# Sliding-window attention and spectral mixing on one core: ACT fills half of the late banks of the tail, and the first halves of four weight groups are read in 8 KB runs

## The chip, the cores and the metric

The kernel runs on one core of one Trainium2 chip. The metric is the device time of one execution in microseconds (us). Before the change it is 430.06 us, the median of three runs (429.9 to 430.35). A profiled execution of the same kernel took 430.23 us; its instructions span 428.4 us of that.

## The reference

Two operators follow each other, on eight batches of 576 tokens, eight heads of 64 (512 channels in all).

```python
mask = (rel >= 0) & (rel < 64)                 # each token sees itself and 63 before it
x = softmax(where(mask, q @ k.T / 8, -1e9)) @ v     # heads side by side: [8, 576, 512]
X = rfft(x, axis=1)[:, :64]                    # 64 modes of the sequence
Yr = Xr @ w_r - Xi @ w_i;  Yi = Xr @ w_i + Xi @ w_r  # each mode its own 512 x 512 matrices
y = irfft(Y, n=576)
u = x + y
out = u + maximum(u @ w_ch, 0)
```

The mode weights w_r and w_i are 64 matrices of 1 MB each in fp32, 134 MB together. All of them have to be read once.

## The kernel before, in words

**Order of the work.** The program is written out by hand in issue order for each engine (`tc.manual_schedule()`); semaphores come from the use of tiles. In the first stage, attention runs over 40 units (lines 510 to 545): PE turns q, k and v (L298, L310), makes scores (L337, L345), subtracts the maximum (L357), turns the probabilities (L365) and multiplies by v (L385). A DFT of each batch (L408) leaves X in `XQ[0]` (first 256 channels) and `XQ[1]` (other 256).

**Weights.** POOL issues every weight load as a DMA that casts fp32 to bf16 (`load_weights`, lines 157 to 215). The 16 groups have four modes each. Groups 0 to 9 come in halves of 256 input channels: `steps` first has the first halves (hb = 0) of groups 0 to 9, then their second halves, then groups 10 to 15 by pairs of modes with all 512 channels. A load of a half group and of w_r or w_i has 1 MB after the cast. Usually one DMA brings it (L203), with two rows of 512 numbers side by side for each partition and mode: 4 KB read, 2 KB written in a run. For the second halves of groups 2 to 9 (`WIDE = 2`), two DMAs of 512 KB bring it (L195), each of two modes, with four rows side by side: 8 KB read, 4 KB written. The other form needs X with the channels spread in another way over the partitions: `wide_modes` (lines 721 to 745) does that for `XQ[1]` with matmuls by a spread identity, and leaves it in `XE`. The loads go into rings of tiles (`ringA`, `ringB`, of three and five buffers), into `Yall` and into some lent tiles. POOL issues them in order, among the raw loads of q, k and v (L285), and a load waits for its buffer to be spent by PE.

**Mode matmuls.** `mode_half` (L223) has 8 matmuls for w_r and 8 for w_i, four of them side by side on PE in 32 columns each. `mode_wide` (L235) also has 8 and 8, two side by side in 64 columns each. The first halves (L223, in `early_step`, lines 536 to 543) run inside the attention stage, in its iterations 22, 23, 24, 26, ... 38; ACT keeps their sums in `Yacc` (L542). After attention, the second halves and then the pairs of groups 10 to 15 (`mode_pair`, L254) run as their weights land, with the product x w_ch (`x_jobs`) and the inverse DFT of what is complete between them.

**The tail.** When the last weights have landed, 36 output tiles of 128 tokens are left, as 18 pairs in the list `seq`. Pairs of the first four batches (list `AA`, "early") have their sums over all modes but the last prepared in `UE`, and need only 32 rows for the last modes (`late_z` L986, `late_u` L979). The others (list `BB`, "late") need all modes (`rows_z` L1050, `rows_u` L1021). `X4` are two late pairs with the last 64 tokens of two batches in one tile; their u matmuls are in two column halves (L1027), their last modes in 32 rows (L1047, L1033). A round of the last loop (lines 1195 to 1198) does for pair n on PE: put x w_ch into two banks (`tail_xw`, L966, a matmul by the identity), add z (`summed`); ACT takes the relu in place (L1074); then for pair n-1 PE adds u into the same bank, DVE adds what is missing and writes the output tile (L1085, L1039), and SP sends it (L996). There are four sets of two banks.

**Warm-up.** PE starts with `WARM` = 59 small matmuls on zeros (L432) while the first k and q are loaded.

Of the kernel before, what the change touches and what calls it, by code (L numbers as in the profile page):

```python
# [16 lines left out]

NRA = 3
NRB = 5
WARM = 59  # L20
NEG = -1.0e30
MAGIC = 12582912.0
PSAFE = 3.14159
# [3 lines left out]
def kernel(  # L27
# [75 lines left out]
    XA = XA[:, 0:(3 * NW + 2) * B * NMF].rearrange("p (s b m) -> p s b m", b=B, m=NMF)  # L103
    steps += [(grp, hb) for grp in (*range(EARLY, LAST), *range(LAST + 2, NGRP), LAST, LAST + 1) for hb in range(2)]
    WIDE = 2
    NE = 2 * (EARLY - WIDE)
    SHARES = 25, 11, 80, 12
    assert sum(SHARES) == 128
    XE = XE[:, 0:(7 * NW + 2) * B * NE].rearrange("p (s b m) -> p s b m", b=B, m=NE)
    ONES = 3, 0  # L110
    wlist = []
    for at, (grp, hb) in enumerate(steps):
# [37 lines left out]
    def load_weights(n):  # L150
        nonlocal nload
        while nload < len(wlist):
            at, parts, hb, ri = wlist[nload]
            if 2 * n <= sum(len(ps) for ps in parts):
                return
            if nload in lent:
                w = lent[nload]
            else:
                open_to = "a" if at >= 2 * EARLY else "aby" if at < EARLY + 2 else "ab"
                h = min(open_to, key=lambda h: held[h][0] if len(held[h]) == room[h] else -1)  # L160
                if len(held[h]) == room[h]:
                    if held[h][0] not in spent:
                        return
                    held[h].pop(0)
                held[h].append(nload)
                if h == "y":
                    w = lentY
                else:
                    w = {"a": ringA, "b": ringB}[h].tile([128, 4, NJ, DM], BF16, name="wi" if ri else "wr", tag="wt")
            src = moe_w_i if ri else moe_w_r  # L170
            if at >= 2 * EARLY:
                w = w.rearrange("p (m h) j e -> p m (h j) e", m=2)
                p = parts[0][0]
                if nload == wstart[2 * EARLY]:
                    row = 0
                    for i, size in enumerate(SHARES):
                        for m in [slice(0, 2)] if i < 2 else [slice(0, 1), slice(1, 2)]:
                            nc.gpsimd.dma_start(
                                out=w[row:row + size, m],
                                in_=src[p:p + 2][m].rearrange("m (p j) e -> p m j e", j=NW)[row:row + size])  # L180
                        row += size
                else:
                    for m, k, lo, hi in ((0, 1, 0, NW), (1, 1, 0, NJ), (1, 1, NJ, NW)) if nload == len(wlist) - 1 else ((0, 2, 0, NW),):
                        nc.gpsimd.dma_start(  # L184
                            out=w[:, m:m + k, lo:hi],
                            in_=src[p + m:p + m + k].rearrange("m (p j) e -> p m j e", j=NW)[:, :, lo:hi])
                wtiles.update(((p + m, ri), w[:, m]) for m in range(2))
                nload += 1
                n -= 2
                continue  # L190
            if at >= EARLY + WIDE:
                w = w.rearrange("p (q h) j e -> p q (h j e)", q=2)
                for i in range(2):
                    p = parts[0][2 * i]
                    nc.gpsimd.dma_start(  # L195
                        out=w[:, i], in_=src[p:p + 2, HALF:DM, :].rearrange("h (p j) e -> p h (j e)", j=NW))
                    wtiles[p, hb, ri] = w[:, i].rearrange("p (j e) -> p j e", j=NW)
                nload += 1
                n -= 4
                continue  # L200
            to = 0
            for ps in parts:
                nc.gpsimd.dma_start(  # L203
                    out=w[:, to:to + len(ps)],
                    in_=src[ps[0]:ps[-1] + 1, HALF * hb:HALF * hb + HALF, :].rearrange("g (p j) e -> p g j e", j=NJ))
                for i, p in enumerate(ps):
                    wtiles[p, hb, ri] = w[:, to + i]
                to += len(ps)
            nload += 1
            n -= to  # L210
# [20 lines left out]
    def mode_wide(psm, at, ri):  # L231
        grp, hb = steps[at]
        for j in range(NW):
            for i in range(2):
                nc.tensor.matmul(out=psm[64 * i:64 * i + 64, :],  # L235
                                 lhsT=XE.rearrange("k s b m -> k (s b) m")[:, (7 * j + 1 - ri) * B:(7 * j + 9 - ri) * B,
                                                                           2 * (grp - WIDE) + i],
                                 rhs=wtiles[4 * grp + 2 * i, hb, ri][:, j], start=(ri == 0 and j == 0),
                                 stop=(ri == 1 and j == NW - 1), tile_position=(0, 64 * i))
        for i in range(2):  # L240
            wtiles.pop((4 * grp + 2 * i, hb, ri))
        spend(at, ri)

    def mode_pair(psm, at, ri):
        grp, h = steps[at]
# [16 lines left out]
    with tc.manual_schedule():  # L262
# [2 lines left out]
        trigF = maskp.tile([128, NTF, 2 * NM], BF16, name="trigF")  # L265
        mask_t = maskp.tile([128, 3, 4, 128], BF16, name="mask_t")
        rawp = pool("rawp", bufs=2)
        qtp = pool("qtp", bufs=3)
        vtp = pool("vtp")
        vdp = pool("vdp")  # L270
# [264 lines left out]
        def early_step(it):  # L535
            nonlocal step
            grp = step
            psm = ps_m.tile([128, DM], FP32, name="psm", tag="misc")
            for ri in range(2):
                mode_half(psm, grp, ri)  # L540
                load_weights(due(it) - loaded())
            nc.scalar.copy(out=Yacc[grp], in_=psm)  # L542
            step += 1
# [55 lines left out]
        trigX = zpool.tile([128, 128], BF16, name="trigX")  # L599
        trigXr = zpool.tile([128, 128], FP32R, name="trigXr")  # L600
        XL = zpool.tile([128, 3 * NW + 2, B, 8], BF16, name="XL")
        sprE = XL.rearrange("p s b m -> p (s b m)")[:, 0:512].rearrange("p (r h k) -> p r h k", r=2, h=2)
        trpool = pool("trpool", bufs=2, reuse_waits="tile")

        banks = {"m": pool("ps_mc", bufs=2, space=PSUM, reuse_waits="tile"),
# [113 lines left out]
                    nc.vector.tensor_scalar(out=XA[:, i], in0=px[:, 1], scalar1=-1.0, scalar2=None, op0=ALU.mult)  # L719

        def wide_modes():
            nc.vector.memset(sprE, 0.0)
            for r in range(2):
                for h in range(2):
                    nc.vector.tensor_copy(out=sprE[:, r, h, h::2], in_=ident_bf[:, r::2])
            pts = [[bank("zt"[r == 0]) for j in range(NJ)] for r in range(2)]
            for r in range(2):
                for j in range(NJ):
                    for h in range(2):
                        nc.tensor.matmul(  # L730
                            out=pts[r][j][:, 2 * B * NE * h:2 * B * NE * (h + 1)], lhsT=sprE[:, r, h],
                            rhs=XQ[1][:, 3 * j + 1:3 * j + 3, :, 4 * WIDE:4 * EARLY].rearrange(
                                "p t b (m h) -> p (t b) m h", h=2)[:, :, :, h],
                            start=(h == 0), stop=True, skip_group_check=True)
            nc.vector.memset(XE[:, 0:7 * NW].rearrange("p (j s) b m -> p j s b m", s=7)[:, :, 3], 0.0)
            nc.vector.memset(XE[:, 7 * NW:], 0.0)
            for r in range(2):
                for j in range(NJ):
                    i = 7 * (NJ * r + j)
                    px = pts[r][j].rearrange("p (h t b m) -> p h t b m", h=2, t=2, b=B)  # L740
                    xe = [XE[:, i + t:i + t + 8].rearrange("p (h s) b m -> p h s b m", h=2) for t in range(2)]
                    nc.scalar.copy(out=xe[1][:, :, 0:2], in_=px)
                    nc.vector.tensor_scalar(out=xe[0][:, :, 0], in0=px[:, :, 1], scalar1=-1.0, scalar2=None, op0=ALU.mult)
            lo = 4 * (LAST - EARLY)
            nc.vector.tensor_copy(out=XL, in_=XA[:, :, :, lo:lo + 8])

# [205 lines left out]
        BB = [(8, 17), (26, 35)] + [(i, i + 1) for k in range(NLB // 2, B // 2) for i in range(9 * k, 9 * k + 8, 2)]  # L952
        assert sorted(i for p in AA + BB for i in p) == list(range(NT))
        X4 = [BB.pop(0) for _ in range(2)]
        seq = [AA.pop(0) for _ in range(4)]
        while AA:
            seq += [BB.pop(0), AA.pop(0)]
        seq += X4 + BB
        ps, pu = {}, {}
        plan = [i for n, p in enumerate(seq) for i in (p if n else p[::-1])]  # L960
        done = {}

        def tail_xw(n, js=(0, 1)):
            for i in [seq[n][j] for j in js]:
                ps[i] = bank(("tt", "yp", "zz", "mm")[n % 4][seq[n].index(i)])
                nc.tensor.matmul(out=ps[i], lhsT=ident_r, rhs=XW[i], start=True, stop=True)  # L966

        def banks_u(n, of):
            for j, i in enumerate(seq[n]):
# [225 lines left out]
        for n in range(2, end):  # L1195
            tail_xw(n)
            summed(n)
            added(n - 1)
        banks_u(end, ("tt", "yp", "zz", "mm")[(end + 1) % 4])
        ut = new_ut()  # L1200
# [39 lines left out]
```

## Time and profile before

| what | before |
|---|---|
| median of three runs | 430.06 us |
| the profiled execution | 430.23 us |
| its span, first to last instruction | 428.4 us |
| PE busy | 336.4 us (79%) |
| DVE busy | 245.7 us (57%) |
| ACT busy | 185.7 us (43%) |
| POOL busy | 90.6 us (21%) |
| moved by all DMA queues | 93.29 MB, mean 218 GB/s |
| weights' queue (software, from POOL) | 31424 packets, 81.80 MB |
| HBM read | 163.58 MB |
| chain that ended last | DMA 49%, PE 37%, issue 4%, DVE 4%, ACT 4%, POOL 1% |

The page of the profile lists busy times, the span in 40 slices (each 10.7 us), the queues, the chain that ended last, the costliest groups and the DMA issues. Bytes of a casting DMA are counted as written (bf16). In the timeline and in the chain, the columns are the start in us from the first instruction, the length in us, engine, line and tiles; what stands in brackets is how long the engine stood idle before and what ended that. In groups, the last number of "x8 | 4.3, 582" is the mean length of one in ns. A windows row gives the stretch, each engine's busy us with the number of instructions, the granted PE clock, the share of the DMA engines and GB/s.

### The profile page before, as it was taken

The page shows a single profiled execution, that of the slowest core. Times are in us where ns is not written, and L with a number is a line of the kernel's source. Part 1 is how long each engine was busy: PE and PEld are TensorE (multiplying, and loading weights), DVE is VectorE, ACT ScalarE, POOL GpSimd, SP SyncE. Part 2 cuts the span into 40 slices and gives each one's busy share as a digit, 9 for nine tenths or more (in the row PEclk, how much of TensorE's full clock was granted, in tenths as well). Part 3 has the DMA queues.
Part 4 walks back from the last instruction along what each step waited for, and adds up shares of the span by engine and source line. Part 5 has one row for each costly group of instructions (what it writes and reads, how often), then busy time and mean ns, then how long its engine had stood idle before and what let it go on. Part 6 is the DMA issues. An engine that isn't in the chain of part 4 may idle for free.

```text
span 428.4 us, 11528 instructions
## 1 busy us (share of the span) xinstructions
PE 336.4 (79%) x5000; PEld 226.7 (53%) x5043; DVE 245.7 (57%) x525; ACT 185.7 (43%) x337; POOL 90.6 (21%) x156
## 2 busy tenths in 40 slices
PE   6898999898999988976627567668676767878994
PEld 5676767676667766662315334345454545445442
DVE  8498887778677765785402212133322334885886
ACT  6575757575676657533301101124222213323772
POOL 8222213122122132112222222211111111120200
PEclk8699999999999999996656888689998998999998
DMA  8999999999999999999999999999999999996797
GB/s 202 212 212 211 211 212 211 212 211 211 211 212 211 212 212 212 211 213 214 213 251 222 213 214 214 206 215 215 214 214 215 215 214 214 214 211 117 264 356 283
DMA packets 37187, 93.29 MB, mean 218 GB/s; under 512 B 2992, under 2 KB 3248, under 8 KB 37136
## 3 DMA queue, kind: packets, MB, share of 16 engines
q0 software_dynamic: 31424, 81.80, 97.8%
q1 hardware_dynamic: 5568, 10.62, 6.8%
q8 instruction: 39, 0.64, 0.5%
q10 hardware_dynamic: 144, 0.13, 0.1%
q14 instruction: 12, 0.10, 0.1%
HBM read 163.58 MB, written 9.44 MB: 404 GB/s over the span
## 4 chain that ended last, share of the span: by engine, by line
DMA 49%; PE 37%; issue 4%; DVE 4%; ACT 4%; POOL 1%; DVEq 0%; ACTq 0%; POOLq 0%
DMA wr<-in_moe_w_r_dram 26%; DMA wi<-in_moe_w_i_dram 23%; PE tr L298 5%; PE s L345 4%; PE s L357 4%; PE pt L365 3%; PE vb L310 3%; PE o L385 2%; PE s L337 2%; PE psz L685 2%; PE psm L254 1%; DVE xw L890 1%; PE psm L223 1%; DMA vd<-in_k_dram 1%; PE px L408 1%
## 5 line engine op out<-in xcount | busy, mean ns | idle before, releaser
L685 PE MATMUL psz<-wch,tr 128*128 128x512 f32 x176 | 57.8, 457 | 10.8 <-DMA wch<-in_moe_w_ch_dram 10.1
L944 DVE CAST xw<-psz 128x512 fp32r<-128x512 f32 x36 | 24.9, 692 | 68.6 <-PE psz L685 68.1
L349 DVE TENSOR_REDUCE mx<-s 128x4 fp32r<-128x512 f32 x72 | 49.4, 687 | 24.7 <-PE s L345 24.4
L653 ACT CAST tr<-ptx 128x512 fp32r<-128x512 bf16 x36 | 21.2, 590 | 80.4 <-PE ptx L678 80.4
L359 ACT ACTIVATE p<-s 128x512 bf16<-128x512 f32 x72 | 39.7, 603 | 12.4 <-PE s L357 12.4
L685 PEld LDWEIGHTS psz<-wch,tr 128*128 128x128 f32 x176 | 34.2, 215 | 17.4 <-issue 10.3
L345 PE MATMUL s<-kT,qT 64*64 64x128 bf16 (+1 forms) x576 | 29.5, 223 | 6.9 <-issue 6.9
L302 ACT COPY kT<-tr 128x576 bf16<-128x576 bf16 x32 | 23.2, 724 | 23.8 <-PE tr L298 23.8
L235 PEld LDWEIGHTS <-XQ 128*64 128x64 bf16 x128 | 14.1, 203 | 30.7 <-issue 25.1
L345 PEld LDWEIGHTS <-qT 64*64 64x64 bf16 x576 | 18.3, 108 | 18.1 <-issue 17.6
L302 ACT COPY qT<-tr 128x576 bf16<-128x576 bf16 x32 | 23.3, 728 | 10.0 <-PE tr L298 10.0
L368 DVE COPY pts<-pt 128x1024 bf16<-128x1024 bf16 (+1 forms) x40 | 25.2, 629 | 3.9 <-PE pt L365 2.3
L357 PE MATMUL s<-mx,ident_r 128*128 128x512 f32 x72 | 26.9, 445 | 0.1
L254 PEld LDWEIGHTS <-XQ 128*32 128x32 bf16 x256 | 9.2, 150 | 29.8 <-issue 29.7
L302 ACT COPY vT<-tr 128x576 bf16<-128x576 bf16 x32 | 23.3, 727 | 3.4 <-PE tr L298 3.3
L749 DVE TENSOR_TENSOR stg<-psm,Yfour 128x512 bf16<-128x512 f32 x10 | 6.9, 691 | 30.4 <-PE psm L235 27.3
L235 PE MATMUL psm<-wi,XQ 128*64 128x512 bf16 x64 | 13.6, 494 | 12.2 <-DMA wi<-in_moe_w_i_dram 12.2
L365 PE MATMUL pt<-ident_bf,p 128*128 128x128 bf16 x288 | 23.0, 221 | 0.2 <-DVE pts L368 0.2
L397 DVE TENSOR_TENSOR x_sb<-o,r 128x512 bf16<-128x512 f32 x32 | 22.1, 692 | 1.1
L285 POOL DMA_DIRECT2D rawk<-in_k_dram x15 | 8.1, 538 | 65.1 <-PE tr L298 59.5
L235 PE MATMUL psm<-wr,XQ 128*64 128x512 bf16 x64 | 14.1, 504 | 8.6 <-DMA wr<-in_moe_w_r_dram 7.1
L184 POOL DMA_DIRECT2D wi<-in_moe_w_i_dram x14 | 9.6, 690 | 50.6 <-PE psm L254 29.3
(294 smaller groups left out, 680.4 us busy)
## 6 DMA issues: line engine op xcount, KB each, us to landing
wi<-in_moe_w_i_dram POOLq DMA_DIRECT2D x21, 1024.0 KB, 14.6
wr<-in_moe_w_r_dram POOLq DMA_DIRECT2D x18, 1024.0 KB, 14.1
wi<-in_moe_w_i_dram POOLq DMA_DIRECT2D x17, 512.0 KB, 19.4
wr<-in_moe_w_r_dram POOLq DMA_DIRECT2D x16, 512.0 KB, 19.4
out_dram<-ut SPq DMA_DIRECT2D x29, 256.0 KB, 2.3
rawv<-in_v_dram POOLq DMA_DIRECT2D x16, 288.0 KB, 15.6
rawk<-in_k_dram POOLq DMA_DIRECT2D x15, 288.0 KB, 14.5
rawq<-in_q_dram POOLq DMA_DIRECT2D x15, 288.0 KB, 14.8
```

The lines of the kernel that those rows point to most:

```text
L235: nc.tensor.matmul(out=psm[64 * i:64 * i + 64, :], lhsT=XE.rearrange("k s b m -> k (s b) m")[:, (7 * j + 1 - ri) * B:(7 * j + 9 - ri) * B, ...
L298: nc.tensor.transpose(out=pt[ro, j, :], in_=raw[ro, TH * half + j, :], identity=ident_bf[ro, ro])
L302: nc.scalar.copy(out=to, in_=pt.rearrange("p j n -> p n j"))
L345: nc.tensor.matmul(out=s[ro, t, lo:128], lhsT=lq, rhs=kT[ro, 64 * n - 64 + lo:64 * n + 64], start=False, stop=True, skip_group_check=True)
L349: nc.vector.tensor_reduce(out=mx, in_=s, axis=AX.X, op=ALU.max, negate=True)
L357: nc.tensor.matmul(out=s, lhsT=ident_r, rhs=mx.unsqueeze(2).to_broadcast([128, 4, 128]), start=False, stop=True, skip_group_check=True)
L359: nc.scalar.activation(out=p[:, 4 * c2:4 * c2 + 4, :], in_=s, func=ACT_F.Exp, scale=EX_SCALE)
L365: nc.tensor.transpose(out=pt[:, t, :], in_=st[u]["p"][:, t, :], identity=ident_bf)
L368: nc.vector.tensor_copy(out=ps[:, 0:nt, :], in_=pt[:, 0:nt, :])
L397: nc.vector.tensor_tensor(out=xo.rearrange("p c (h d) -> p c h d", d=64), in0=ov[:, :, :, 0:64], in1=rb, op=ALU.mult)
L685: nc.tensor.matmul(out=pz, lhsT=tr[:, c, :], rhs=wch[:, c, :], start=(c == 0), stop=(c == NDCH - 1))
L944: nc.vector.tensor_copy(out=XW[i], in_=multiply(tr))
```

## The change

Three parts.

1. The first halves of groups 6 to 9 (`FIRST_WIDE = 6`) are loaded in the form that the second halves of groups 2 to 9 have: two DMAs of 512 KB with 8 KB runs in place of one of 1 MB with 4 KB runs, for w_r and w_i of each, eight loads in all. `wide_modes` becomes a common function `spread_modes`; it is called for `XQ[0]` in the early step of group 5, inside attention, with two banks of the pool `ps_m`, and leaves X in a new tile `XF`. The early steps of groups 6 to 9 use `mode_wide`. The spread identity is now one tile of 257 columns, read at two offsets, filled by one memset and two copies in place of one and four.
2. In the tail, x w_ch of the second tile of pairs n = 4, 6, ... 16 is put into its bank by ACT (`copy_xw`), after the relus of round n-2, instead of by PE in round n. The two pairs `X4` go from places 12 and 13 of `seq` to places 8 and 10.
3. `WARM` goes from 59 to 51.

In the changed program PE issues 8 warm-up matmuls and 7 of L966 fewer, and 16 matmuls of 128 columns more in the early step of group 5. ACT issues 4 copies more there and 7 in the tail. DVE issues two memsets and four scalings for `XF`, one memset and two copies for the spread identity. POOL issues 8 DMAs more, SP none.

```diff
-WARM = 59
+WARM = 51
...
+    FIRST_WIDE = 6
+    wide_from = (FIRST_WIDE, WIDE)
...
-            if at >= EARLY + WIDE:
+            if steps[at][0] >= wide_from[hb]:
                 w = w.rearrange("p (q h) j e -> p q (h j e)", q=2)
                 for i in range(2):
                     p = parts[0][2 * i]
                     nc.gpsimd.dma_start(
-                        out=w[:, i], in_=src[p:p + 2, HALF:DM, :].rearrange("h (p j) e -> p h (j e)", j=NW))
+                        out=w[:, i],
+                        in_=src[p:p + 2, HALF * hb:HALF * hb + HALF, :].rearrange("h (p j) e -> p h (j e)", j=NW))
...
+    def spread_modes(hb, spread, pts):
+        xe, m0 = XE[hb], wide_from[hb]
+        n = 2 * (EARLY - m0)
+        nc.vector.memset(spread, 0.0)
+        for r in range(2):
+            nc.vector.tensor_copy(out=spread[:, 128 * r + 1:128 * r + 128:2], in_=ident_bf[:, r::2])
+        for r in range(2):
+            for j in range(NJ):
+                px = pts[r][j].rearrange("p (h x) -> p h x", h=2)
+                for h in range(2):
+                    nc.tensor.matmul(
+                        out=px[:, h], lhsT=spread[:, 128 * r + 1 - h:128 * r + 129 - h],
+                        rhs=XQ[hb][:, 3 * j + 1:3 * j + 3, :, 4 * m0:4 * EARLY].rearrange(
+                            "p t b (m h) -> p (t b) m h", h=2)[:, :, :, h],
+                        start=(h == 0), stop=True, skip_group_check=True)
...
+                nc.scalar.copy(out=at[1][:, :, 0:2], in_=px)
+                nc.vector.tensor_scalar(out=at[0][:, :, 0], in0=px[:, :, 1], scalar1=-1.0, scalar2=None, op0=ALU.mult)
...
         def early_step(it):
+            if grp == FIRST_WIDE - 1:
+                both = [ps_m.tile([128, DM], FP32, name="spread", tag="misc") for r in range(2)]
+                spread_modes(0, spread, [[t[:, HALF * j:HALF * j + HALF] for j in range(NJ)] for t in both])
             psm = ps_m.tile([128, DM], FP32, name="psm", tag="misc")
             for ri in range(2):
-                mode_half(psm, grp, ri)
+                (mode_half if grp < FIRST_WIDE else mode_wide)(psm, grp, ri)
...
         X4 = [BB.pop(0) for _ in range(2)]
+        BB = BB[0:2] + X4 + BB[2:]
         seq = [AA.pop(0) for _ in range(4)]
         while AA:
             seq += [BB.pop(0), AA.pop(0)]
-        seq += X4 + BB
+        seq += BB
...
+        copied = {seq[n][1] for n in range(4, len(seq) - 1, 2)}
...
+        def copy_xw(n):
+            i = seq[n][1]
+            if i in copied:
+                ps[i] = bank_z(n, 1)
+                nc.scalar.copy(out=ps[i], in_=XW[i].bitcast(FP32))
...
             tail_xw(n)
             summed(n)
+            if n + 2 < end:
+                copy_xw(n + 2)
             added(n - 1)
```

More of the change, by code (lines that the diff above doesn't have):

```diff
@@ L108 @@
     assert sum(SHARES) == 128
-    XE = XE[:, 0:(7 * NW + 2) * B * NE].rearrange("p (s b m) -> p s b m", b=B, m=NE)
+    XE = {1: XE[:, 0:(7 * NW + 2) * B * NE].rearrange("p (s b m) -> p s b m", b=B, m=NE)}
     ONES = 3, 0
@@ L235, in mode_wide @@
                 nc.tensor.matmul(out=psm[64 * i:64 * i + 64, :],
-                                 lhsT=XE.rearrange("k s b m -> k (s b) m")[:, (7 * j + 1 - ri) * B:(7 * j + 9 - ri) * B,
-                                                                           2 * (grp - WIDE) + i],
+                                 lhsT=XE[hb].rearrange("k s b m -> k (s b) m")[:, (7 * j + 1 - ri) * B:(7 * j + 9 - ri) * B,
+                                                                               2 * (grp - wide_from[hb]) + i],
                                  rhs=wtiles[4 * grp + 2 * i, hb, ri][:, j], start=(ri == 0 and j == 0),
@@ L242, in mode_wide @@
         spend(at, ri)
+    def spread_modes(hb, spread, pts):
[13 more added lines that the diff above has]
+                        start=(h == 0), stop=True, skip_group_check=True)
+        nc.vector.memset(xe[:, 0:7 * NW].rearrange("p (j s) b m -> p j s b m", s=7)[:, :, 3], 0.0)
+        nc.vector.memset(xe[:, 7 * NW:], 0.0)
+        for r in range(2):
+            for j in range(NJ):
+                i = 7 * (NJ * r + j)
+                px = pts[r][j].rearrange("p (h t b m) -> p h t b m", h=2, t=2, b=B)
+                at = [xe[:, i + t:i + t + 8].rearrange("p (h s) b m -> p h s b m", h=2) for t in range(2)]
+                nc.scalar.copy(out=at[1][:, :, 0:2], in_=px)
+                nc.vector.tensor_scalar(out=at[0][:, :, 0], in0=px[:, :, 1], scalar1=-1.0, scalar2=None, op0=ALU.mult)
     def mode_pair(psm, at, ri):
@@ L267 @@
         rawp = pool("rawp", bufs=2)
+        NF = 2 * (EARLY - FIRST_WIDE)
+        XE[0] = maskp.tile([128, 7 * NW + 2, B, NF], BF16, name="XF")
+        spread = maskp.tile([128, 257], BF16, name="spread")
         qtp = pool("qtp", bufs=3)
@@ L601 @@
         XL = zpool.tile([128, 3 * NW + 2, B, 8], BF16, name="XL")
-        sprE = XL.rearrange("p s b m -> p (s b m)")[:, 0:512].rearrange("p (r h k) -> p r h k", r=2, h=2)
+        sprE = XL.rearrange("p s b m -> p (s b m)")[:, 0:257]
         trpool = pool("trpool", bufs=2, reuse_waits="tile")
@@ L721, in wide_modes @@
         def wide_modes():
[L722 to L743, printed above, removed]
+            spread_modes(1, sprE, [[bank("zt"[r == 0]) for j in range(NJ)] for r in range(2)])
             lo = 4 * (LAST - EARLY)
@@ L961, with bank_z @@
         done = {}
+        copied = {seq[n][1] for n in range(4, len(seq) - 1, 2)}
+        def bank_z(n, j):
+            return bank(("tt", "yp", "zz", "mm")[n % 4][j])
         def tail_xw(n, js=(0, 1)):
-            for i in [seq[n][j] for j in js]:
-                ps[i] = bank(("tt", "yp", "zz", "mm")[n % 4][seq[n].index(i)])
-                nc.tensor.matmul(out=ps[i], lhsT=ident_r, rhs=XW[i], start=True, stop=True)
+            for j in js:
+                i = seq[n][j]
+                if i not in copied:
+                    ps[i] = bank_z(n, j)
+                    nc.tensor.matmul(out=ps[i], lhsT=ident_r, rhs=XW[i], start=True, stop=True)
+        def copy_xw(n):
[3 more added lines that the diff above has]
+                nc.scalar.copy(out=ps[i], in_=XW[i].bitcast(FP32))
         def banks_u(n, of):
```

## The prediction

> **What bounds the kernel now.** I read the page first, for the stretches in which the transfers are full.
>
> ```profile
> span 428.4 us, 11528 instructions
> ...
> PE   6898999898999988976627567668676767878994
> ...
> DMA  8999999999999999999999999999999999996797
> GB/s 202 212 212 211 211 212 211 212 211 211 211 212 211 212 212 212 211 213 214 213 251 222 213 214 214 206 215 215 214 214 215 215 214 214 214 211 117 264 356 283
> ```
>
> A slice is 10.7 us. The transfer engines are full from the start to the 36th slice (about 390 us), and what they move is almost constant. The last four slices are another stage, the tail, in which the output goes out. Second, the chain of waits, to see who sets the end of each stage.
>
> ```profile
> 143.02 23.23 DMA wr<-in_moe_w_r_dram
> ...
> 169.76 27.70 DMA wr<-in_moe_w_r_dram
> ...
> 340.87 13.71 DMA wi<-in_moe_w_i_dram
> 354.61 0.69 PE psm L254 x16
> ...
> 382.65 11.11 DMA wi<-in_moe_w_i_dram
> ...
> 393.79 0.44 PE psm L254 x4
> ...
> 405.41 0.67 PE psm L966 x2
> 406.08 0.43 PE psm L986 x2
> 406.51 0.54 PE psz L1021 x2
> 407.05 0.47 PE pst L966 x2
> 407.51 0.47 PE pst L1050 x2
> 407.98 0.32 PE psm L979 x2
> 408.30 0.44 PE psy L966
> ```
>
> Columns are start, length, what. From 143 us to 393.8 us the chain is mostly weights landing. Stretches of compute stand in it (after 354.61), but a queue that is full all the time moves the last byte at the same moment whoever is named. Then it is PE nearly without a break: the seven rows from 405.41 on are two rounds of the tail, and they repeat. A round makes two output tiles; rounds alternate between an early pair (32-row matmuls L986, L979) and a late pair (L1050, L1021). Two rounds take 408.30 - 405.41 = 2.89 us, all of it PE. So there are two prices: bytes per us until 393.8, PE per round after.
>
> **The packets of groups 6 to 9.** Eight loads of 1 MB (wr and wi of four groups) become two DMAs of 512 KB each, with 4 KB instead of 2 KB written per packet. Bytes are the same. Two answers of the DMA view show queue 0 (packets, MB, share), the first from 20 to 170 us, where the packets are of 2 KB and of 2.25 KB (raw q, k, v), the second from 226 to 258 us, where all are of 4 KB.
>
> ```profile
> q0 software_dynamic: 15602, 31.29, 110.8%
> ```
>
> ```profile
> q0 software_dynamic: 1880, 6.82, 106.1%
> ```
>
> That is 31.29 MB / 150 us = 208.6 GB/s against 6.82 / 32 = 213.1. The eight loads are 8.39 MB: 40.2 us at the first rate, 39.4 at the second, so 0.85 us less. A stretch with 2 KB packets almost alone, 172 to 191 us, bounds it from the other side:
>
> ```profile
> q0 software_dynamic: 1978, 3.99, 111.4%
> ```
>
> 3.99 / 19 = 210.0 GB/s, so 40.0 us, and 0.6 us less. I take 0.8, nearer to the long window.
>
> The Trainium skill, page "DMA: Bandwidth & Descriptors", section "Specifications", says that transfers of 512 B and more run at line rate. By that rule 2 KB and 4 KB packets are equal and this term is 0. The rows above differ by 1.5 to 2.2%, so the trace speaks against it.
>
> **What the new form costs in the attention stage.** A half-width step (L223) has 16 matmuls, four of them side by side; a wide one (L235) has 16, two side by side.
>
> ```profile
> 139.05 1.11 PE psm L223 x14
> ...
> 276.30 1.04 PE psm L235 x7
> ```
>
> 16 of the first take 16/14 x 1.11 = 1.3 us, of the second 16/7 x 1.04 = 2.4 us: 1.1 us more in each of four groups, 4.4 us. The re-laying of X is that of the second half, which the trace shows:
>
> ```profile
> 200.64 0.27 DVE L722 MEMSET XL<- 128x256 uint32 x1
> ...
> 203.73 2.11 PE L235 MATMUL psm<-wr,XQ 128*64 128x512 bf16 x8 [1.46 <-DVE XQ L743]
> ```
>
> From its first memset to the first wide matmul 3.1 us pass. The new one has half the columns but takes both "misc" banks in the middle of attention, and the half-width step of group 5 queues behind it on PE, so I take 3 us again. PE, at 8 to 9 tenths there (first 17 slices of its row), ends attention 7 us later.
>
> This is hidden if queue 0 stays full. The load issued at 169.76 us lands 27.7 us later, at 197.46. The next ones wait for PE:
>
> ```profile
> 178.28 1.19 POOL L195 DMA_DIRECT2D wi<-in_moe_w_i_dram  x2 [7.30 <-PE psm L223]
> ```
>
> They are needed in the queue only shortly before the earlier bytes end. Of the 27.7 us some 5 are start and receipt (a final 512 KB at 213 GB/s takes 2.5), so the queue would run dry near 192 us: 14 us of cover for 7 us of delay. More DMAs also make POOL itself wait, as here, for the one of 160.79 us, eight DMAs back:
>
> ```profile
> 190.63 0.58 POOL L195 DMA_DIRECT2D wi<-in_moe_w_i_dram  x1 [4.60 <-DMA Yall<-in_moe_w_r_dram]
> ```
>
> But eight of 512 KB are still 19 us of bytes, and raw loads handed over later keep their place behind the same bytes. Cost 0; without the cover each us beyond 14 costs one us. After 190 us PE's row has holes (2 to 7 tenths) in which it catches up.
>
> The 8 fewer warm-up matmuls cost nothing: after the last PE idles 2.06 us for the cast of k.
>
> ```profile
> 6.57 0.47 PE L298 MATMUL tr<-ident_bf,rawk 64*64 64x64 bf16 x18 [2.06 <-DVE rawk L426]
> ```
>
> The shorter setting up of L722 and L725 (two copies for four) lies beside the same full queue: 0.
>
> Does the end follow the queue? PE waits for the last piece, and little else holds it:
>
> ```profile
> 393.79 0.44 PE L254 MATMUL psm<-wi,XL 128*32 128x256 bf16 x4 [0.81 <-DMA wi<-in_moe_w_i_dram]
> ```
>
> The compute burst ahead of it begins with a landing (the wi issued at 340.87, landed at 354.6), so it moves along with the queue. I count the whole 0.8.
>
> **The tail, copies.** ACT fills the bank of the second tile in seven late rounds (n = 4, 6, ... 16), so seven L966 matmuls go. In a run of like matmuls two take 0.47 us (407.05), so one is 0.235: 7 x 0.235 = 1.6 us. What is late next is ACT:
>
> ```profile
> 404.89 1.07 ACT L1074 ACTIVATE psz<-psz 128x512 f32<-128x512 f32 x2 [0.17 <-PE psz L1050]
> 406.54 1.07 ACT L1074 ACTIVATE psm<-psm 128x512 f32<-128x512 f32 x2 [0.57 <-PE psm L986]
> 407.78 0.58 ACT L1074 ACTIVATE pst<-pst 128x512 f32<-128x512 f32 x1 [0.18 <-PE pst L1050]
> ```
>
> The copy of round n+2 stands between these two. The hole is 0.57 us, and PE now comes 0.23 sooner: 0.34 is left. Two relus take 1.07 and one 0.58, so the pitch is 0.49. The trace has no ACT copy from SBUF to PSUM. Its bounds are that 0.49 and the ACT operation that reads SBUF:
>
> ```profile
> L636 ACT ACTIVATE MtI<-Qi x1: 682/682/682, 210.5 to 210.5; 128x576 f32<-128x576 f32 x1
> ```
>
> With 0.5 the relus behind it come 0.16 us late. Queued behind them: on PE the u matmuls of that round (L979, L1021), which stand behind the next round's xw and z matmuls. The relu of 406.54 ends at 407.61 and its L979 starts at 407.98 on the chain, so 0.3 us of slack swallows most; I give back 0.06 each, 0.4 together. Copies: -1.2. With 0.68, two rounds of ACT (2.14 + 0.68 = 2.82) stand against 2.89 before: only 0.5 is won. The copy's bank was emptied by DVE a round before, so it waits for nothing.
>
> ```profile
> 406.87 1.29 DVE L1039 TENSOR_TENSOR ut<-psz,x_sb 128x512 f32<-128x512 f32 x2
> ```
>
> DVE's two adds of a round take 1.29, two rounds at most 2.58: not the bound.
>
> **The tail, last tokens' pairs.** They go from rounds 12 and 13 to 8 and 10, behind early pairs.
>
> ```profile
> 411.87 0.43 PE psm L986 x2
> 412.30 0.54 PE psz L1021 x2
> 412.83 0.46 PE pst L966 x2
> 413.29 0.32 PE pst L1047
> 413.62 0.20 PE psm L979
> 413.81 0.42 PE psy L966
> ```
>
> Round 12 now takes 413.81 - 412.83 = 0.98 us against 1.25 of a usual late round (407.05 to 408.30), as its 32-row z matmuls go beside the 32-row u matmuls of the early pair. Both pairs get such a place, one more than now: -0.27. The odd u matmuls of these pairs move along unchanged. I take -0.3, between 0 and -0.6.
>
> Output is no wall: one slice of 1 us shows what the queue can do.
>
> ```profile
> 402.00:403.00 1.00, 1.00 (x5) 0.39 (x4) 0.90 (x2) 1.00 (x3) 0.00 (x0) 1.00 1.06 389
> ```
>
> 36 tiles of 262 KB at 389 GB/s are 24.3 us; 34.6 us lie between the last weights (393.8) and the end. Tail: -1.5, between -0.4 and -1.9.
>
> **Sum.** -0.8 - 1.5 = -2.3 us. The profiled execution took 430.23 us (428.4 of span, 1.8 around it): 427.9. The median of the three runs is 0.17 lower, so 427.8.
>
> **Rivals.**
> *The packets give nothing*: the slower rate of 20 to 170 us is due to raw loads and instruction fetches, not to packet size. For it: the window nearest to pure 2 KB packets is already at 210.0. Against: that is still under 213.1. Then only the tail counts: 428.6. Chance 0.13. By the rule of the Trainium skill's DMA page on 512 B this is what would come.
> *ACT becomes the tail's bound*: a copy at 0.68 leaves -0.5 there, so -1.3 in all: 428.8. Against: relus from PSUM are 0.58 long. Chance 0.14.
> *Slower: the queue runs dry behind attention.* Place: POOL's loads that wait for PE near 170 to 190 us. It decides from 14 us of delay, twice my 7; it outweighs the 2.3 won from about 16. At 18 us the price is 4, net +1.7: 431.8. For it: PE is 9 tenths busy there and the two banks block the transposes too. Chance 0.08.
> *No effect*: the copies only move the tail's wait to ACT or DVE and the packets give little, within 0.9 us of 430.06. Chance 0.07.
>
> **How the numbers follow.** Forecast 0.58, the rivals 0.13, 0.14, 0.08, 0.07. The likeliest is 427.8. The range holds the first three: low end -0.9 - 1.9 = -2.8, 427.2; high end -0.4 for the tail alone, 429.7. This kernel's measurement tells about 0.2%, 0.86 us, from no change. Faster by more: 0.58 + 0.13 + 0.13 = 0.84 (the last 0.01 of the second rival falls within); within: 0.07 + 0.01 = 0.08; slower: 0.08.
>
> **What would show it.** The last psm L254 starts near 393.0, not 393.8; queue 0 moves its bytes in 102 to 172 us at over 209 GB/s; PE's attention matmuls end some 7 us later and no slice before 390 us falls under 205 GB/s. In the tail a late round has one L966 and two rounds take about 2.7 us; the copy's mean is near 0.58 and ACT's hole before the early pair's relus is gone. A last psm at 393.8, a copy over 0.7 or a slice under 200 GB/s near 190 us would prove the steps wrong.

## The result and the profile after

The changed kernel takes **428.67 us**, the median of six runs (428.25 to 429.05). Six runs of the kernel before beside them gave 430.3 us (429.9 to 431.93). The ratio is 0.996, with a 95% interval of 0.9949 to 0.9972: 1.2 to 2.2 us faster, more than the 0.2% that a measurement of this kernel can tell. The profiled execution took 428.67 us, with 426.9 us of span, against 430.23 and 428.4 before.

The page of after, first the same rows as before's:

```profile
span 426.9 us, 11528 instructions
...
PE   5898998898999789996717557677767667878993
...
DMA  8999999999999999999999999999999999996698
GB/s 208 211 212 213 210 212 211 212 211 211 213 212 213 213 213 211 212 213 214 212 250 225 213 215 214 204 213 215 215 215 215 213 214 214 215 215 135 231 372 304
```

The queue is full through the same slices, and no slice before the tail falls under 204 GB/s, just below the 205 that the forecast named; before had 206 in the same place. So nothing ran dry behind attention. In the tail the slice of 372 GB/s is new (356 before). Next the chain of waits of after (start, length, what):

```profile
382.44 10.82 DMA wi<-in_moe_w_i_dram
...
393.30 0.44 PE psm L282 x4
...
402.08 0.43 PE psy L987
...
403.70 0.23 PE psz L987
...
404.72 0.66 PE psm L987 x2
...
407.33 0.44 PE psy L987
...
415.32 1.07 ACT psz L1101 x2
416.39 0.50 ACT pst L993
...
418.34 0.59 ACT pst L1101
...
421.44 1.26 DVE ut L1123 x3
```

The stage of the weights ends 0.49 us earlier (393.79 before). A late round now has one identity matmul (403.70), and two rounds take 404.72 - 402.08 = 2.64 us, then 407.33 - 404.72 = 2.61, against 2.89. But the tail as a whole, from 393.30 to the end of the span, is 33.57 us against 34.65 (to the hundredth, the spans end at 426.87 and 428.44): only 1.08 shorter. From 415.3 to 418.1 us ACT stands on the chain, where before it is PE until 419.7.

How ACT looks inside: its timeline, and the groups of the copies in the tail (mean ns behind the comma).

```profile
404.21 1.07 ACT L1101 ACTIVATE psz<-psz 128x512 f32<-128x512 f32 x2
405.18 0.60 ACT L993 COPY pst<-xw 128x512 f32<-128x512 f32 x1
405.83 1.07 ACT L1101 ACTIVATE psm<-psm 128x512 f32<-128x512 f32 x2
```

```profile
L993 ACT COPY pst<-xw 128x512 f32<-128x512 f32 x4 | 2.4, 603 | 0.0
...
L993 ACT COPY psz<-xw 128x512 f32<-128x512 f32 x3 | 1.8, 607 | 0.0
```

A copy takes 0.60 us, nearly the relu's 0.58, and never waits. The hole of 0.57 us ahead of the early pair's relus is filled.

In what follows two marks are read from the chain of each run: **the tail**, from the first of the last four weights' matmuls to the end of the span, and **the sums**, from there to the end of DVE's last sum (after: 421.44 + 1.26 - 393.30 = 29.40; before: 423.32 + 1.26 - 393.79 = 30.79, the last row of its chain). The second leaves out the sending of the last output. Tails of other runs are from the span's end to the hundredth, too.

```profile
423.32 1.26 DVE ut L1096 x3
```

### The profile page after: what moved, and what is told of

It is laid out like the page before. It is cut to its first block, busy times and chain, and to the rows that moved or that the text cites. A ratio compares the mean times of both kernels' runs of the same rounds, so it can differ in the third digit from the quotient of the medians.

```text
span 426.9 us, 11528 instructions
## 1 busy us (share of the span) xinstructions
PE 335.4 (79%) x4993; PEld 229.6 (54%) x5036; DVE 246.6 (58%) x532; ACT 190.4 (45%) x348; POOL 94.1 (22%) x164
## 4 chain that ended last, share of the span: by engine, by line
DMA 47%; PE 37%; DVE 5%; issue 5%; ACT 4%; POOL 1%; DVEq 0%; ACTq 0%; POOLq 0%
DMA wi<-in_moe_w_i_dram 23%; DMA wr<-in_moe_w_r_dram 19%; PE tr L329 6%; PE s L376 4%; DMA rawq<-in_q_dram 4%; PE s L388 3%; PE pt L396 3%; PE vb L341 3%; PE o L416 2%; PE psz L719 2%; PE s L368 2%; PE psm L282 2%; PE psm L226 2%; DVE xw L903 1%; PE psm L238 1%
## 5 line engine op out<-in xcount | busy, mean ns | idle before, releaser
L957 DVE CAST xw<-psz 128x512 fp32r<-128x512 f32 x36 | 24.9, 692 | 72.0 <-PE psz L719 71.5
L380 DVE TENSOR_REDUCE mx<-s 128x4 fp32r<-128x512 f32 x72 | 49.4, 687 | 24.8 <-PE s L376 24.4
L719 PEld LDWEIGHTS psz<-wch,tr 128*128 128x128 f32 x176 | 34.6, 218 | 18.1 <-issue 11.3
L197 POOL DMA_DIRECT2D wi<-in_moe_w_i_dram x22 | 12.8, 584 | 44.0 <-DMA wi<-in_moe_w_i_dram 18.3
L197 POOL DMA_DIRECT2D wr<-in_moe_w_r_dram x24 | 14.1, 590 | 32.9 <-DMA wr<-in_moe_w_r_dram 20.6
L186 POOL DMA_DIRECT2D wi<-in_moe_w_i_dram x14 | 9.5, 684 | 50.4 <-PE psm L282 33.8
```

Source lines behind the costliest of these rows:

```text
L197: nc.gpsimd.dma_start(out=w[:, i], in_=src[p:p + 2, HALF * hb:HALF * hb + HALF, :].rearrange("h (p j) e -> p h (j e)", j=NW))
L380: nc.vector.tensor_reduce(out=mx, in_=s, axis=AX.X, op=ALU.max, negate=True)
L719: nc.tensor.matmul(out=pz, lhsT=tr[:, c, :], rhs=wch[:, c, :], start=(c == 0), stop=(c == NDCH - 1))
L957: nc.vector.tensor_copy(out=XW[i], in_=multiply(tr))
```

## The experiments

The times stand beside runs of the kernel before on the same chip. Marks, bytes and chains are from one profiled execution of each kernel, and are compared with those of before and after above.

**Packets alone.** After's part 1 on the kernel before.

```diff
-WARM = 51
+WARM = 59
...
-        BB = BB[0:2] + X4 + BB[2:]
...
-        seq += BB
+        seq += X4 + BB
...
-        copied = {seq[n][1] for n in range(4, len(seq) - 1, 2)}
+        copied = set()
```

> The kernel before with the first part of the change alone (first halves of groups 6 to 9 in 4 KB written packets, their X re-laid inside attention); tail and warm-up as before. The forecast's theory, 0.1 us less per load of 1 MB: 0.8 us faster, 429.5, last weights' matmuls starting near 393.0. The theory from the trace of after (last weights' matmuls 393.30 against 393.79 there): 0.5 us faster, 429.8. The rival that packets give nothing, and that the 0.49 us in the trace of after was chance between two executions: 430.3, last weights at 393.8. That the re-laying costs something behind attention: slower than 430.3, with a stretch of queue 0 under 200 GB/s near 190 us.

Measured: 429.72 us (11 runs) against 430.09 (33 runs), ratio 0.9993 (0.9984 to 1.0002): 0.37 us faster by the medians, with an interval that includes no change and just leaves out the forecast's 0.8 (0.9981). Its one trace has the last weights at 392.90, which would be 0.89 faster. That is misleading, and the next views show why. Queue 0 (packets, MB, share) from 0 to 20 us, before and then the packets alone:

```profile
q0 software_dynamic: 1438, 2.92, 80.4%
```

```profile
q0 software_dynamic: 1486, 3.01, 82.0%
```

This execution was 0.09 MB, or 0.4 us, ahead before any changed load. From 20 to 102 us both move the same, 17.10 MB:

```profile
q0 software_dynamic: 8535, 17.10, 110.8%
```

```profile
q0 software_dynamic: 8532, 17.10, 110.8%
```

And from 102 to 172 us, where the eight loads are, before moves 14.60 MB, the packets alone 14.68 and after 14.69:

```profile
q0 software_dynamic: 7272, 14.60, 110.7%
```

```profile
q0 software_dynamic: 5404, 14.68, 107.5%
```

```profile
q0 software_dynamic: 5416, 14.69, 107.6%
```

0.08 to 0.09 MB at 14.60 / 70 = 208.6 GB/s are 0.4 us. Followed packet by packet in the trace, the lead over before grows by 0.25 to 0.33 us in after and by 0.19 to 0.36 in the packets alone, by where the marks are set (18 to 42 MB, 18 to 46, 6 to 38). In 102 to 172 us the four other kernels with part 1 below move 14.68 or 14.69 MB too, and those without it 14.58 to 14.62. So **eight loads are worth some 0.3 us, 0.04 each**, not 0.1.

**The opposite, on 12 other loads.**

```diff
-    WIDE = 2
+    WIDE = 8
```

(and the re-laying reads only the columns that are left).

> The kernel before with the opposite of the first part, on other loads and half as many again: the second halves of groups 2 to 7, which before reads in 8 KB runs, go back to 4 KB read and 2 KB written (12 loads of 1 MB); only groups 8 and 9 stay wide. Nothing else changes; PE has 1.1 us less work in each of six groups. The price per load of the forecast, 0.1 us: 1.2 us slower, 431.5. The price by the trace of after, 0.06 us: 0.7 us slower, 431.0. Packets give nothing: 430.3 or a little less.

Measured: 430.34 us (11 runs) against 430.09, ratio 1.0007 (0.9998 to 1.0016): 0.25 us slower, with an interval that includes no change and leaves out 1.2 us. Queue 0 from 172 to 258 us, before and then narrow:

```profile
q0 software_dynamic: 6334, 18.76, 107.9%
```

```profile
q0 software_dynamic: 9187, 18.67, 112.1%
```

0.09 MB less is 0.4 us, 0.035 a load: the same price on other loads, with the other sign. And the forecast's own window, 226 to 258 us, now with half-size packets for 5.90 of the 6.81 MB:

```profile
q0 software_dynamic: 3222, 6.81, 111.7%
```

6.81 MB, where before moves 6.82 in packets of 4 KB. The 208.6 GB/s of the attention stage were therefore not the rate of 2 KB packets. The lines above queue 0's in the two answers that the forecast used, 20 to 170 us and 226 to 258 us of before, count all queues together:

```profile
DMA packets 15631, 31.72 MB, mean 211 GB/s; under 512 B 968, under 2 KB 968, under 8 KB 15602
```

```profile
DMA packets 1881, 6.84 MB, mean 214 GB/s; under 512 B 208, under 2 KB 208, under 8 KB 1880
```

In the first window 0.43 MB of instruction fetches go beside queue 0, in the second 0.02. With them, 31.72 / 150 = 211.5 GB/s stand against 6.84 / 32 = 213.8, and the forecast's sum for 8.39 MB gives 0.4 us, not 0.85. That the fetches take the place of weights byte for byte is an estimate; no run took them away.

**More DMAs, same packets.** The first halves of groups 6 to 9 in two DMAs of 512 KB with 4 KB read and 2 KB written.

```diff
             to = 0
+            if hb == 0 and 6 <= steps[at][0] < EARLY:
+                parts = [ps[i:i + 2] for ps in parts for i in (0, 2)]
             for ps in parts:
```

> The kernel before with the first halves of groups 6 to 9 loaded by two DMAs of two modes each, as the change does, but in runs as before: 4 KB read, 2 KB written. Read by the time at which the weights' queue has moved its first 42 MB less the time for its first 18 MB, against the same in before: -0.33 us in after and -0.26 in the packets alone (to 46 MB -0.25 and -0.19; from 6 to 38 MB -0.27 and -0.36). If the size of the packets does it: 0.0, within 0.1. If the cutting into more DMAs does it: -0.3.

Measured by these marks: +0.08 us from 18 to 42 MB, +0.17 from 18 to 46, +0.15 from 6 to 38 (one run, 430.12 us beside 429.77). From 102 to 172 us:

```profile
q0 software_dynamic: 7390, 14.58, 110.8%
```

14.58 MB against 14.60. Cutting alone wins nothing, it loses 0.1 to 0.2 us. The gain comes with the larger packets.

**Copies alone.**

```diff
+        copied = {seq[n][1] for n in range(4, len(seq) - 1, 2)}
...
             tail_xw(n)
             summed(n)
+            if n + 2 < end:
+                copy_xw(n + 2)
             added(n - 1)
```

> The kernel before with the copies by ACT alone; the two pairs of last tokens stay in rounds 12 and 13, weights and warm-up as before. The forecast: seven matmuls of 0.235 us go, 0.4 us are given back to ACT, so 1.2 us faster, 429.1. ACT as the bound (2.82 us of ACT in two rounds against 2.89 of PE): 0.5 faster, 429.8. By the trace of after, where the tail is 1.0 us shorter with both parts: 0.7 to 1.0 faster, 429.3 to 429.6.

**Moved pairs alone.**

```diff
         X4 = [BB.pop(0) for _ in range(2)]
+        BB = BB[0:2] + X4 + BB[2:]
...
-        seq += X4 + BB
+        seq += BB
```

> The kernel before with the two pairs of last tokens moved from rounds 12 and 13 to 8 and 10, and nothing else. The forecast: one more round in which their 32-row z matmuls go beside 32-row u matmuls, 0.3 us faster, 430.0. If what limits the last rounds is not PE (ACT, or the transfers of the output): no change, 430.3, within 0.15.

Measured: copies 429.14 us, ratio 0.9977 (0.9968 to 0.9985), 0.95 us by the medians; pairs 429.81, ratio 0.999 (0.9981 to 0.9999), 0.28 us (11 runs each, against the same 430.09). With the packets' 0.37 these make 1.60 of the 1.63 that after wins, so nothing that these runs can tell is left for the warm-up. It wasn't tried alone, but PE's first transpose starts at 6.57 us with 51 warm-up matmuls as with 59. The chains of the copies and of the pairs:

```profile
393.95 0.44 PE psm L254 x4
...
422.32 1.26 DVE ut L1109 x3
```

```profile
393.86 0.44 PE psm L254 x4
...
423.08 1.26 DVE ut L1097 x3
```

| kernel | sums | tail |
|---|---|---|
| before | 30.79 | 34.65 |
| copies alone | 29.63 | 33.84 |
| moved pairs alone | 30.48 | 34.36 |
| after | 29.40 | 33.57 |

The sums came in as forecast: 1.16 us earlier with the copies (1.2), 0.31 with the pairs (0.3), 1.39 with both (1.5). The tail did not follow: with both it is 1.08 shorter, with the copies 0.81. Some 0.3 us are lost between the last sum and the end, in both.

**Which copies count.** After with the first four copies alone, and with the last three alone:

```diff
-        copied = {seq[n][1] for n in range(4, len(seq) - 1, 2)}
+        copied = {seq[n][1] for n in range(4, 12, 2)}
```

```diff
-        copied = {seq[n][1] for n in range(4, len(seq) - 1, 2)}
+        copied = {seq[n][1] for n in range(12, len(seq) - 1, 2)}
```

> The kernel after with only the first four copies by ACT (rounds 4, 6, 8, 10); in rounds 12, 14 and 16 PE's matmul is back. Read by the tail, from the first of the last four weights' matmuls to the end of the span: 34.65 us before, 33.57 after, 34.36 with the moved pairs alone, so seven copies are worth 0.79 or 0.11 each. If each copy is worth the same: 33.9. If the last rounds are held by ACT or by the transfers of the output anyway, the last three copies are worth nothing: 33.6. If PE sets the pace to the end and a matmul costs its 0.235: 34.3.

> The kernel after with only the last three copies by ACT (rounds 12, 14 and 16). Tail, measured as in the run beside it. If each copy is worth 0.11: 34.0. If the last three are worth nothing: 34.35, as with the moved pairs alone. If the output's transfers have room once the early rounds are no faster than before, and a matmul saved is worth its 0.235: 33.65.

The first four: 429.17 us, ratio 0.9966 (0.9954 to 0.9979), not to be told from after. Its profiled execution was 3.6 us longer than its median, so its trace isn't used, and this experiment decides nothing. The last three, one run of 428.52:

```profile
392.77 0.44 PE psm L282 x4
...
421.40 1.26 DVE ut L1123 x3
```

Sums 29.89, tail 33.98, as expected if each copy is worth the same: three copies bring 0.38 us of the 0.79 that seven bring to the tail (34.36 with the moved pairs alone, 33.57). That they are worth nothing, because the last rounds are held up anyway, is refuted.

**Half of the output.** Every second tile is not sent, in after and in before.

```diff
-                put_out(nc.sync, plan.pop(0), 0, DM)
+                i = plan.pop(0)
+                if i % 2:
+                    put_out(nc.sync, i, 0, DM)
```

> The kernel after, but every second output tile (the even ones) is not sent, so half of the output is left out; all sums are made as before. That the transfers of the output hold the end back by their queue (the last tile lands 2.8 us after its issue, against 2.1 us for a lone one): tail 32.8 in place of 33.57, DVE's last sum unchanged at 29.4 us after the last weights. That ACT or PE alone holds it: 33.4 to 33.6.

> The kernel before with the same half of the output left out. The queue's theory: the last tile's 2.56 us come down to 2.1, tail 34.2 in place of 34.65, so that with half the output the change's tail part is worth 1.4 us, not 1.08. The theory of ACT or PE alone: both lose the same, and the difference stays at 1.08.

The chains, after's and then before's:

```profile
393.17 0.44 PE psm L282 x4
...
421.31 1.26 DVE ut L1125 x3
```

```profile
394.24 0.44 PE psm L254 x4
...
423.76 1.26 DVE ut L1098 x3
```

One run each took 427.45 and 429.90 us. The sums are unmoved, 29.40 and 30.78. The tails are 32.51 and 33.88, 1.06 and 0.77 shorter; both are 0.3 under the expectation of the queue's theory, their difference is the one expected. With half of the output the change is worth 1.37 us in the tail, all that the sums won; with the whole output 1.08. **The transfers of the output took the other 0.3 us.** It lies behind the last sum: with the whole output the last piece lands 2.81 us after its issue in after and 2.56 in before, with half of it 2.06 in both. The answer of the DMA view for 398 to 432 us says how (KB of one, median us from issue to landing), for before, after, and after with half of the output:

```profile
out_dram<-ut SPq DMA_DIRECT2D x29, 256.0 KB, 2.3
```

```profile
out_dram<-ut SPq DMA_DIRECT2D x29, 256.0 KB, 2.5
```

```profile
out_dram<-ut SPq DMA_DIRECT2D x15, 256.0 KB, 2.0
```

With half of the output a tile needs 2.0 us. In after the tiles queue.

**Half of the relu.** ACT's relu in the tail's rounds covers 256 of 512 columns, in after and in before.

```diff
-                nc.scalar.activation(out=ps[i], in_=ps[i], func=ACT_F.Relu)
+                nc.scalar.activation(out=ps[i][:, 0:HALF], in_=ps[i][:, 0:HALF], func=ACT_F.Relu)
```

> The kernel after, with the relu of the tail's rounds on the first 256 columns alone, so the relu of the other half is left out: ACT gets some 0.4 us free per round, everything else stays. Read by DVE's last sum after the last weights, 29.40 us in after. If ACT holds what the copies give back (seven matmuls of 0.235 us are 1.65, the chain of sums won 1.15 with the copies alone): DVE's last sum at 28.9. If PE or DVE holds it: 29.3 to 29.4.

> The kernel before with the same half of the relu left out. DVE's last sum is at 30.78 us after the last weights there. If PE alone sets the pace without the copies, as the chain of before shows: 30.7 to 30.8. If ACT's relus already hold PE's u matmuls back in before: 30.4 or less, and then the half relu in after tells less.

Chains, after's and then before's:

```profile
393.43 0.44 PE psm L282 x4
...
420.51 1.26 DVE ut L1123 x3
```

```profile
393.54 0.44 PE psm L254 x4
...
422.41 1.26 DVE ut L1096 x3
```

Sums 28.34 and 30.13, 1.06 and 0.66 earlier. So ACT's relus already delayed before's sums, which the forecast had not counted, and a part of after's 1.06 is that. The rest, 0.4, is what the change gives back to ACT, if before's share is the same in after: with ACT eased the change is worth 30.13 - 28.34 = 1.79 us of sums, without 1.39. Yet the sharpest reading is the end. In before the tail shrinks with the sums, to 34.02 from 34.65. After's sums come 1.06 us sooner, and its tail is **33.96 us, against 33.57**: nothing of the microsecond reached the end, and with ACT eased the change is worth 0.06 us of tail. One run each took 429.16 us (after) and 429.33 (before). After's output tiles wait longer instead:

```profile
out_dram<-ut SPq DMA_DIRECT2D x29, 256.0 KB, 3.3
```

Queue 1, which carries the output, from 402 to 422 us in before, in after, and in after with half of the relu:

```profile
q1 hardware_dynamic: 3973, 7.22, 98.1%
```

```profile
q1 hardware_dynamic: 4125, 7.51, 101.6%
```

```profile
q1 hardware_dynamic: 4182, 7.61, 102.8%
```

361, 376 and 380 GB/s. The copies alone move 7.61 MB there too. After is within 1.3% of what the kernel with 1.06 us faster sums gets, and no run moves more than 381 GB/s in any 20 us of the tail: 380 is taken for the ceiling here, 0.69 us for each tile of 262 KB. What sets it was not tried.

## Why the prediction was right, and where its sizes were off

The total is 2.3 us forecast against 1.6 measured, and 428.67 lies in the range. The sign, the order of the terms and the two mechanisms, larger packets and fewer PE matmuls in the tail, are right. Both terms came out smaller than forecast, so the hit is no cancelling of errors; one wall was overlooked. Step by step:

- **What bounds the kernel: stands.** The last weights still set the start of the tail, and the queue is never dry.
- **Packets, -0.8: the term was mis-sized; 0.3 to 0.4 measured.** The last weights' matmuls start at 393.30, not near 393.0. The step that failed compared the rates of two windows as if packet size were their only difference. Queue 0 moves 212.8 GB/s at 226 to 258 us with mostly 2 KB packets too (6.81 / 32). Attention's stage also holds raw loads and instruction fetches; counting the fetches brings the forecast's sum down to 0.4, but no run took them away. The lower bound, 0.6, came from another such window (172 to 191 us), so it was no bound. The Trainium skill, page "DMA: Bandwidth & Descriptors", section "Specifications", has all transfers of 512 B and more at line rate; two packet sizes above that differ here by 0.04 us in some 5 (0.8%), so the trace is nearer to that rule than to my price, and still not at zero.
- **Cost inside attention, hidden: right.** The re-laying stops PE for longer than I took, and the wide steps cost less. Three rows of after's timeline and the last one's counterpart in before, the idle time in brackets:

```profile
148.38 0.63 PE L257 MATMUL spread<-XQ,spread 128*128 128x128 bf16 x8 [1.83 <-DVE spread L252]
...
150.29 0.89 PE L226 MATMUL psm<-x_sb,XQ 128*32 128x512 bf16 x8 [1.29 <-DVE XF L270]
```

```profile
198.21 0.69 PE L226 MATMUL psm<-wr,XQ 128*32 128x512 bf16 x8 [0.64 <-ACT XQ L445]
```

```profile
193.69 1.10 PE L223 MATMUL psm<-wr,XQ 128*32 128x512 bf16 x8 [0.64 <-ACT XQ L414]
```

  From the last matmul before the stall (ends 146.55) to 150.29 it is 3.7 us, in which PE works 0.6. The re-laying has 8 matmuls, as the row shows, not the 16 of the section on the change. A wide step of group 6 takes 2.0 us (161.04 to 163.05 in after), the half-width step 1.1 (158.72 to 159.83 in before): 0.9 more, not 1.1. The first mode step after attention starts at 198.21, against 193.69 before: 4.5 us late, not 7, and less than 3.7 and four times 0.9 together, so PE caught up with some of it inside attention. The cover, estimated at 14 us, was enough for 4.5; how far it reaches no run shows.
- **Copies, -1.2: right in its place, and the give-back too.** The sums come 1.16 us earlier, near 7 x 0.235 = 1.65 less the 0.4 that ACT takes. ACT's copy is 0.60 us, between the bounds 0.49 and 0.68.
- **Last tokens' pairs, -0.3: right** (0.31 in the sums, 0.28 in the time).
- **"Output is no wall": wrong, and with it 0.3 us of the tail's 1.5.** The step set 24.3 us of transfers against 34.6 us of tail, as if the output could flow through all of it. In the trace the first output lands 7.5 us after the last weights (issued at 5.2), and the span ends 1.3 us behind the last landing. Between the first and the last landing 25.8 us pass in before, 24.8 in after, 24.6 in the copies alone and 24.9 in after with half of the relu, where the median tile waits longest: the change has used up nearly all that there was to win. The check that was missing is the pace: 4 tiles in the forecast 2.7 us are 388 GB/s, in the measured 2.63 us 399, above the 380 that queue 1 sustains. One slice of 1 us at 389 was taken for a sustained rate.
- **Two rivals came nearer in time than the forecast's 427.8, by luck:** "the packets give nothing" (428.6) and "ACT becomes the tail's bound" (428.8). The first puts the whole miss on the packets, which gave 0.3 us, though its doubt of the window's rate was right. The second puts it on ACT, which takes the 0.4 us that the forecast had counted; its copy is 0.60, not 0.68. What the tail lacks beyond that, the output took.

In all, the traces give 0.3 + 1.1 = 1.4 us and the medians 1.6, with an interval of 1.2 to 2.2 that holds both.

## What to carry to other kernels

Before you shorten a stage that ends in stores, divide the bytes of a round by the new time of a round and hold that against the rate that the store queue sustains over many tiles, not total bytes against total time: start, landing and finish take their share of the stage. Price a transfer's form by swapping that form alone and comparing the same stretch of the same queue, for windows of one profile differ in more than one thing; where you must compare windows, count the bytes of all queues. Where a term is under half a microsecond, compare how leads grow between two marks of the trace: where a single execution ends also carries the offset with which it started.

## What the runs showed of the hardware

- The profiled executions come out of the first 16 us up to 0.6 us apart and then keep that offset: the queue of weights passed its first 2 MB at 15.74 us in before, 0.25 us sooner in after, 0.47 in the packets alone and 0.07 later with the moved pairs alone, and from 6 to 22 MB no offset moved by more than 0.1 us. Whether it is chance is open. The six traces with part 1 of the change are 0.01 to 0.49 us sooner than before (0.36 in the mean), the six others from 0.19 sooner to 0.07 later, although the loads that part 1 changes come later; no run shows why.
- With the output's tiles arriving faster than 0.69 us apart, their landing took 3.3 us in the median against 2.0 for tiles that had the queue to themselves, while the rate stayed at 380 GB/s.
- PE's granted clock (the third number from the end in a row of the windows view, after's row first, then before's) was 0.91 in the 20 us with the re-laying, where PE stood idle for 3 us, and 1.00 in before. Whether the idle time causes it was not tried.

```profile
140.00:160.00 20.00, 16.25 (x323) 11.43 (x327) 13.76 (x37) 10.75 (x20) 5.37 (x10) 0.91 1.08 214
```

```profile
140.00:160.00 20.00, 18.18 (x401) 13.12 (x403) 14.61 (x32) 11.74 (x21) 4.44 (x8) 1.00 1.12 211
```
